# Storing before loading in every second full chunk of a streaming 1x1 convolution

One core of a Trainium2 chip. The metric is the device time of one execution, in microseconds (us), median of several runs.

## The reference

```python
x:  (1, 384, 384, 384) bf16;  dw: (1, 1, 384) bf16;  pw: (384, 384) bf16
out = x * dw[0, 0]                            # k = 1: one factor per channel
return einsum('bhwc,cd->bhwd', out, pw)       # a 147456 x 384 by 384 x 384 product
```

The kernel folds `dw` into `pw` once and then streams `x` through: 113 MB in, 113 MB out.

## The kernel before

The rows are cut into 42 chunks: sizes 1, 1, 2, 4 at the head, thirty-four full chunks of 8 supertiles (512 rows each), and 4, 2, 1, 1 at the tail. Full chunks are t = 4 to 37. VectorE transposes a supertile (X to T), TensorE multiplies it (T to PSUM), ScalarE and VectorE evict it (PSUM to O). SyncE issues all loads and stores of x and of the output, in program order, into one queue. X and O have three buffers each.

```python
LMAX = 8; NX = 3; NO = 3
def load_x(t):                       # chunk t into X[t % NX]
    d = nc.sync.dma_start(Xs[t % NX]..., src)   # je (here and below): the chunk's last supertile; its line is cut
    if t >= NX:                      # waits until chunk t-NX has been transposed
        d._wait_ge(s_t[je % 2][1], je // 2 + 1)
    d.then_inc(s_x[t % NX], 16)
def store(t):                        # O[t % NO] out; waits for the evictions of chunk t
    nc.sync.wait_ge(s_d[je % 2], je // 2 + 2)
    d = nc.sync.dma_start(dst, Os[t % NO]...)
    d._wait_ge(s_a[je % 2], je // 2 + 2)
    d.then_inc(s_o[t % NO], 16)
# ... cut: first loads, weights ...
for t in range(NT):
    if t + NX < NT:
        load_x(t + NX)
    store(t)
# ... cut: matmuls, transposes, evictions.
#     Transposes of a chunk wait for s_x; its first evictions wait for s_o.
```

## Time and profile before

| | before |
|---|---|
| time | 586.65 us, 3 runs (586.26 to 586.95) |
| span of the profile | 584.0 us |
| TensorE, VectorE busy | 97%, 97% |
| DMA | 1.01 of its engines' time from 200 to 300 us, 406 GB/s |

The prediction shows the lines for these. One view it does not show is the list of waits (who waited for whom: us in total, times, longest):

```profile
DVE T L174 <- DMA X<-in_x_dram: 1.6, 2, 1.3
PE ps L134 <- DVE T L174: 1.0, 1, 1.0
```

Read it with the chain: the DMA is as full as TensorE, yet VectorE waits for a load only twice, for 1.6 us. The loads arrive ahead of need.

### The profile page before, as it was taken

To read this page: it belongs to the slowest core of one execution; us is meant where nothing else is said; L and a number is where in the kernel's file an instruction comes from. 1 tells how busy PE (TensorE), PEld (TensorE's weight loads), DVE (VectorE), ACT (ScalarE), POOL (GpSimd) and SP (SyncE) were. 2 spreads that over 40 slices of the span, in tenths; PEclk is the share of its full clock that TensorE was granted. 3 is DMA by queue.
4 is the path that set the end of the run, shared out by engine and by line. 5 is a ranking of instruction groups with operands and counts; after the bars stand their busy time and mean duration, and the time that the engine had idled before them with its cause. 6 is when DMAs were issued, how large, how long until landed. Compare 5 with 4: busy or idle time off the path is not lost.

```text
span 584.0 us, 29852 instructions
## 1 busy us (share of the span) xinstructions
PE 563.9 (97%) x13824; PEld 412.6 (71%) x13824; DVE 563.9 (97%) x876; ACT 326.9 (56%) x297; POOL 0.3 (0%) x5
## 2 busy tenths in 40 slices
PE   1999999999999999999999999999999999999995
PEld 0667777777777777777777777777777777777773
DVE  3899999999999999999999999999999999999995
ACT  3555555555555656565655555555555555555553
POOL 0000000000000000000000000000000000000000
PEclk9999999999999999999999999999999999999998
DMA  8799999999999999999999999999999999999858
GB/s 289 253 424 425 428 422 421 410 396 404 402 396 411 378 412 411 394 402 413 391 407 395 414 414 396 404 419 396 404 397 403 389 424 397 389 403 407 333 221 311
DMA packets 29277, 227.79 MB, mean 390 GB/s; under 512 B 1616, under 2 KB 5456, under 8 KB 24656
## 3 DMA queue, kind: packets, MB, share of 16 engines
q1 hardware_dynamic: 28640, 227.09, 97.1%
q10 hardware_dynamic: 624, 0.59, 0.4%
q14 instruction: 12, 0.10, 0.0%
q8 instruction: 1, 0.02, 0.0%
HBM read 114.43 MB, written 113.25 MB: 390 GB/s over the span
## 4 chain that ended last, share of the span: by engine, by line
PE 93%; DMA 5%; ACT 1%; SPq 0%; issue 0%; DVE 0%; ACTq 0%; DVEq 0%
PE ps L134 93%; DMA X<-in_x_dram 2%; DMA out_dram<-O 1%; DMA pw_r<-in_pw_dram 1%; ACT O L215 1%; ACT w_r L199 1%; DVE T L174 0%; SPq L89 0%; SPq L107 0%; SPq L95 0%; SPq L245 0%; DVEq L173 0%; ACTq L211 0%; ACTq L194 0%; SPq L84 0%
## 5 line engine op out<-in xcount | busy, mean ns | idle before, releaser
L134 PE MATMUL ps<-w_r,T 32*128 32x384 bf16 x13824 | 563.9, 322 | 13.8 <-ACT w_r L199 12.8
L134 PEld LDWEIGHTS ps<-w_r,T 32*128 32x128 bf16 x13824 | 412.6, 93 | 164.8 <-issue 14.4
L215 ACT CAST O<-ps 128x1152 bf16<-128x1152 f32 x288 | 322.2, 1119 | 245.2 <-PE ps L134 243.3
L174 DVE STREAM_TRANSPOSE T<-X 128x384 uint32<-128x384 uint32 x576 | 449.1, 856 | 1.6 <-DMA X<-in_x_dram 1.6
L212 DVE CAST O<-ps 128x384 bf16<-128x384 f32 x288 | 160.7, 558 | 6.8 <-PE ps L134 4.6
L199 ACT ACTIVATE w_r<-pw_r,dwsel 128x384 bf16<-128x384 bf16 x6 | 3.1, 601 | 5.4 <-DMA pw_r<-in_pw_dram 5.4
L186 DVE CAST dwsel<-dwt 32x12 f32<-32x12 bf16 x4 | 0.7, 163 | 3.9 <-DMA dwt<-in_dw_dram 3.8
L197 DVE TENSOR_SCALAR w_r<-pw_r,dwsel 128x384 bf16<-128x384 bf16 x6 | 1.5, 312 | 2.1 <-DMA pw_r<-in_pw_dram 2.1
L160 ACT ACT_TABLE_LOAD x1 | 1.3, 1283 | 2.3 <-issue 2.3
L157 DVE MEMSET seed<- 128x1 f32 x2 | 0.1, 59 | 1.0 <-SPq L84 1.0
L160 ACT COPY warm<-warm 128x1 f32<-128x1 f32 x2 | 0.3, 190 | 0.0
L234 POOL MEMSET const-bfloat16-1.0<- 128x1 bf16 x1 | 0.1, 102 | 0.0
L234 POOL MEMSET const-uint8-127<- 128x1 uint8 x1 | 0.1, 101 | 0.0
L158 POOL MEMSET warm<- 128x3 f32 x1 | 0.1, 100 | 0.5 <-SPq L84 0.5
L234 POOL MEMSET const-float32-0.0<- 128x1 f32 x1 | 0.1, 98 | 0.2 <-issue 0.2
L234 POOL MEMSET const-float32-1.0<- 128x1 f32 x1 | 0.1, 98 | 0.0
## 6 DMA issues: line engine op xcount, KB each, us to landing
X<-in_x_dram SPq DMA_DIRECT2D x34, 3072.0 KB, 17.9
out_dram<-O SPq DMA_DIRECT2D x34, 3072.0 KB, 23.0
X<-in_x_dram SPq DMA_DIRECT2D x2, 1536.0 KB, 12.4
out_dram<-O SPq DMA_DIRECT2D x2, 1536.0 KB, 13.5
X<-in_x_dram SPq DMA_DIRECT2D x4, 384.0 KB, 5.7
X<-in_x_dram SPq DMA_DIRECT2D x2, 768.0 KB, 10.1
out_dram<-O SPq DMA_DIRECT2D x4, 384.0 KB, 3.8
out_dram<-O SPq DMA_DIRECT2D x2, 768.0 KB, 11.3
```

What stands on the lines that cost most here:

```text
L134: mm = nc.tensor.matmul(PS[s][:, q, :D], lhsT=Ts[s][32 * q : 32 * q + 32, b, par::2], rhs=w_r[32 * q : 32 * q + 32, b, par, :], start=(b = ...
L157: nc.vector.memset(seed[:, s : s + 1], 0.0).then_inc(s_d[s])
L158: nc.gpsimd.memset(warm[:], 0.0).then_inc(s_seed)
L160: c = nc.scalar.copy(warm[:, s + 1 : s + 2], warm[:, 0:1])
L174: ins = nc.vector.transpose(out=Tw[:, 3 * h : 3 * h + 3], in_=Xw[:, :, j, 96 * h : 96 * h + 96].rearrange("p k (b w) -> p b k w", w=32),)
L186: nc.vector.tensor_copy(dwsel[32 * q : 32 * q + 32, :], dwt[:].rearrange("w b r -> w (b r)")).then_inc(s_ds)
L197: i = nc.vector.tensor_scalar_mul(w_r[:, b, r, :], pw_r[:, b, r, :], sc)
L199: i = nc.scalar.activation(w_r[:, b, r, :], pw_r[:, b, r, :], COPY, scale=sc)
L212: e = nc.vector.tensor_copy(Ov[:, 3, j, :], PS[s][:, 3, :D])
L215: a = nc.scalar.copy(Ov[:, 0:3, j, :], PS[s][:, 0:3, :D])
L234: nc = _bacc.Bacc("TRN2", target_bir_lowering=False, num_devices=1)
```

## The change

The intent: two transfers of one kind follow each other in the queue, so there are half as many switches between reading and writing HBM. For full chunks with even t the store is issued first.

```diff
         for t in range(NT):
+            late = chunks[t] == LMAX and t % 2 == 0
+            if late:
+                store(t)
             if t + NX < NT:
                 load_x(t + NX)
-            store(t)
+            if not late:
+                store(t)
```

The queue's order goes from L S L S to S L L S S L L S. The even chunks' loads, called late loads below, stand behind the store's waits.

## The prediction

> **What bounds the kernel now.** I read the page first (busy shares, the chain that ended last, the groups), then the chain in order of time, the windows (is the DMA full?), SyncE's own timeline (when is each transfer issued?), and the DMA view window by window (when does each land?). The chain says where the end comes from:
>
> ```profile
> span 584.0 us, 29852 instructions
> PE 563.9 (97%) x13824; PEld 412.6 (71%) x13824; DVE 563.9 (97%) x876; ACT 326.9 (56%) x297; POOL 0.3 (0%) x5
> PE 93%; DMA 5%; ACT 1%; SPq 0%; issue 0%; DVE 0%; ACTq 0%; DVEq 0%
> L134 PE MATMUL ps<-w_r,T 32*128 32x384 bf16 x13824 | 563.9, 322 | 13.8 <-ACT w_r L199 12.8
> ...
> 31.44 538.40 PE ps L134 x13248
> ...
> 571.01 7.67 DMA out_dram<-O
> ```
>
> From 31.44 to 569.84 us the chain is nothing but matmuls: one unbroken piece of 538.40 us. The group's idle column says the same: 13.8 us of idle in all, 12.8 of them before the weights were scaled at the start. So the steady state is paced by TensorE (VectorE, 97% busy, turns with it), and not by any transfer. But the DMA has nothing to spare either:
>
> ```profile
> 200.00:300.00 100.00, 100.00 (x2468) 73.47 (x2464) 100.00 (x154) 57.55 (x52) 0.00 (x0) 1.00 1.01 406
> ```
>
> The last two columns are the DMA share and GB/s: 1.01 and 406 in the middle of the run (398 to 424 in the windows from 60.6 to 500). The demand is one full load and one full store (3072 KB each, 6.29 MB together) per full chunk of 15.60 us, or 403 GB/s. Two resources are full; only one of them ends the run. What lies between them is buffer slack, so I measured it. SyncE's timeline for chunks 34 (first two lines), 35 and 36:
>
> ```profile
> 513.43 0.33 SPq L95 DMA_DIRECT2D X<-in_x_dram  x1
> 516.41 0.39 SPq L107 DMA_DIRECT2D out_dram<-O  x1
> 529.03 0.33 SPq L95 DMA_DIRECT2D X<-in_x_dram  x1
> 532.01 0.39 SPq L107 DMA_DIRECT2D out_dram<-O  x1
> 544.63 0.33 SPq L95 DMA_DIRECT2D X<-in_x_dram  x1
> 547.61 0.39 SPq L107 DMA_DIRECT2D out_dram<-O  x1
> ```
>
> The load of chunk t+3 goes out at a moment I call a, when chunk t's transposes end; the store of chunk t follows 2.98 us later, when its evictions end. The pair repeats every 15.60 us. In the DMA view (size, us from issue to landing), window 44.5 to 60.1 (chunk 4), then 512.5 to 528.1 (chunk 34):
>
> ```profile
> X<-in_x_dram SPq DMA_DIRECT2D x1, 3072.0 KB, 13.6
> out_dram<-O SPq DMA_DIRECT2D x1, 3072.0 KB, 18.9
> ```
> ```profile
> X<-in_x_dram SPq DMA_DIRECT2D x1, 3072.0 KB, 20.0
> out_dram<-O SPq DMA_DIRECT2D x1, 3072.0 KB, 25.4
> ```
>
> Landings drift from 13.6 to 20.0 (loads) and from 18.9 to 25.4 (stores) over 30 chunks, about 0.21 us per chunk. The transfers are slower than TensorE by that much, 15.8 us a pair against 15.6, and the three-deep buffers absorb it. A load issued at a is wanted when chunks t+1 and t+2 have been transposed, at a + 31.2; it lands at a + 20.0 at worst, 11.2 us early. A store frees a buffer wanted about 32 us after its issue (the next writer of that buffer is three chunks on); it lands after 25.4 at worst, some 6.6 us early. That is why VectorE waits on loads for 1.6 us in the whole run, at the start and in the tail.
>
> **What the Trainium skill says.**
> 1. "Perfetto Trace Analysis", section Identifying the Most-Contended Engine: matmul busy time is no good measure of headroom, because matmuls are pipelined. So I don't rest on the 97%, but on the missing idle time and the fixed rhythm (evictions start every 1.95 us, at 291.02, 292.97, 294.92). The trace agrees: 322 ns for one matmul, while 48 of them take 1.95 us.
> 2. "DMA: Bandwidth & Descriptors", section Queues, rings and completion order: on each DMA engine descriptors are consumed in ring order, and a transfer is complete only when every engine it uses has reported. The trace agrees as far as it goes: every store lands after the load issued 2.98 us before it (at 2.98 + 25.4 = 28.4 against 20.0 for chunk 34, 8.4 us apart).
> 3. Same page, section Where 436 GB/s comes from: a ceiling of 435 GB/s for a core's DMA. The highest window reads 424, so halving the switches between loads and stores has at most some 3% to win on the DMA itself (estimate, 435/424), 8% against the demand of 403.
> 4. I found no page that puts a price on a switch from reading to writing HBM within a queue. The prediction has to get by without one.
>
> **The change, part by part.** Nothing is removed or added: 42 loads and 42 stores, with the same bytes, waits and buffers; TensorE, VectorE and ScalarE keep their instruction order. Only SyncE's order changes, for full chunks with even t: t = 4, 6, ... 36, 17 of the 34. The sequence L S L S becomes S L L S S L L S.
> - *The moved loads.* Load t+3 now stands behind the store's two waits, so it goes out at a + 2.98 + about 0.4 (the store's issue, 0.39), and in the ring it lies behind 3 MB that used to lie behind it. The bytes up to the end of the pair are the same, so the pair finishes when it did, with the load last: at a + 2.98 + 18.9 = a + 21.9 for chunk 4, and a + 28.4 for chunk 34. That is 8.3 to 8.4 us later than before. The deadline stays a + 31.2. Slack falls from 11.2 to **2.8 us** for the load issued at chunk 34, the worst full one (ready at 541.8, wanted at 544.6). It is 9.3 us at chunk 4. No wait: 0 us.
> - *The moved stores.* They go out at the same time and land earlier by about the time of one load (some 7.5 us, estimate: 3.15 MB at about 420 GB/s). No engine waits for them in the steady state: 0 us.
> - *The odd chunks.* Load t+4 and store t+1 are issued when they were, behind the same bytes as before: 0 us.
> - *Could the queue run dry in the longer gap before an even chunk?* At chunk 4, SyncE issues at 48.41 and the store before it (issued 32.45, 19.3 to land) lands at 51.75. At chunk 6 it issues at 79.61, and the store of chunk 5 (64.01 + 19.4) lands at 83.4. The small first store shows that a landing includes about 2 us that are not transfer (384 KB in 2.9 us), so 1.3 to 1.8 us of work are still queued at the leanest places, and more later. No dry spell: 0 us.
> - *The last moved load* (chunk 36, 768 KB) now lands no later than where store 36 landed, 547.61 + 16.5 = 564.1; it is wanted when chunk 38 is transposed, at 568.03 (SyncE issues the next load then). 3.9 us to spare: 0 us.
> - *The tail.* From 560.23 on the issues are the same in order and content. The 2.2 us that VectorE waits for a store near the end (and ScalarE 1.9) stay.
>
> Sum: 0 us, hence the time of before, 586.65, with a small allowance upward for the thin slack: **586.8 us**.
>
> **The rivals.**
> *A: fewer switches make the DMA faster.* For it: the DMA is full (1.01), and its landings drift. Against it: no compute engine waits for it between 31.44 and 569.84, so a faster DMA only ends the drift. It can shorten the wait for the last stores (7.67 us on the chain, of which ScalarE's idle before its last eviction is 1.9). At most about 2 us: 584.5.
> *B: the thin slack breaks.* If the new order makes a pair slower by more than 2.8/30 = 0.09 us, the loads of even chunks come late near the end and VectorE waits. The kernel is then DMA-bound, and self-limiting: every further 0.1 us per pair costs some 3 us over 30 pairs. A drift of 0.4 instead of 0.2 us gives about 3 us in waits and up to 3 in the tail: 590 to 592. For it: a margin of 2.8 us in 31.2 is not much, and two stores in a row could pile up at HBM. Against it: the bytes and descriptors are the same, and the three-deep buffers cover it on the measured numbers.
> *C: the change turns the kernel clearly DMA-bound.* Over 2% is 11.7 us, so the pair would have to slow by about (2.8 + 11.7)/30 = 0.48 us, 3% of the DMA's rate. Nothing in the trace points to it. 598 or more.
> *D: the late load stalls at every even chunk.* That would need a landing of over 31.2 us; the estimate is 21.9 to 28.4. It would cost up to some us per even chunk; I give it next to nothing.
>
> **Range and chances.** A gain is capped at 2 us, since TensorE's unbroken 538 us remain; a loss is open, but has to eat the slack first. Runs of before spread from 586.26 to 586.95. So the range is lopsided: 585.4 to 589.0. Faster by over 2% (below 574.9) would take a shorter matmul chain: 1%. Slower by over 2% (above 598.4) is rival C: 3%. Within 2%: 96%.
>
> **What would show it.** In the changed kernel's profile the chain should still hold one piece of about 538 us of matmuls; VectorE's waits on loads should stay near 1.6 us; loads of even chunks should land some 19 to 25 us after their later issue, their stores in about 11 to 18, and odd chunks should keep 13.6 to 20 and 19 to 25. The DMA share should stay at 1.00 with about 403 GB/s. I am wrong if VectorE waits for loads in the last third (B), if those waits come from chunk 7 on (D), if TensorE's piece breaks up and GB/s drop below 395 (C), or if landings stop drifting and the time falls by 1 to 2 us (A).

## The result

594.9 us (4 runs, 593.97 to 594.97) against 586.75 us (4 runs) of the kernel before, a ratio of 1.0136 (95% interval 1.0119 to 1.0154). Ratios here are the mean time of one kernel's fast runs over that of the other's of the same rounds, so not quite the ratio of the medians quoted. The change costs 1.4%: within 2%, but well above the predicted range.

The page of the changed kernel: span, busy shares, and the chain that ended last by engine.

```profile
span 593.2 us, 29852 instructions
PE 565.0 (95%) x13824; PEld 412.8 (70%) x13824; DVE 562.9 (95%) x876; ACT 327.0 (55%) x297; POOL 0.3 (0%) x5
DVE 54%; DMA 25%; PE 15%; issue 4%; ACT 1%; SPq 0%; DVEq 0%; ACTq 0%
```

The busy times are those of before; the span is 9.2 us longer. The chain has left TensorE. Its DVE share must be read with care: TensorE and VectorE run in step, and the chain follows now one, now the other. The new thing is the 25% of DMA. In order of time (start, us, what), the longest DMA pieces late in the chain are:

```profile
361.89 28.79 DMA X<-in_x_dram
393.24 30.00 DMA X<-in_x_dram
425.79 29.49 DMA X<-in_x_dram
...
490.29 29.56 DMA X<-in_x_dram
...
577.17 10.76 DMA out_dram<-O
```

In the kernel before this stretch was one piece of 538.40 us of matmuls. Now the chain goes through late loads, each 28.8 to 30.0 us long, and ends in a store that takes 10.76 us instead of 7.67. The waits:

```profile
DVE T L179 <- DMA X<-in_x_dram: 9.6, 6, 3.6
PE ps L139 <- DVE T L179: 8.6, 7, 3.2
```

VectorE waits 9.6 us for loads, TensorE in turn 8.6 us for VectorE. By the trace, 1.8 us of the 9.6 lie at the start (1.3 in the kernel before), 4.2 between 390 and 520 us, and 3.6 at 584 us, before the last chunk. Where is the time lost? The windows give the DMA share and GB/s in their last columns. The kernel before from 400 to 500 us, then the changed kernel in two windows:

```profile
400.00:500.00 100.00, 100.00 (x2471) 73.52 (x2464) 100.00 (x155) 57.39 (x52) 0.00 (x0) 1.00 1.01 405
```
```profile
200.00:300.00 100.00, 100.00 (x2472) 73.75 (x2464) 100.00 (x155) 57.21 (x52) 0.00 (x0) 1.00 1.01 405
400.00:500.00 100.00, 97.09 (x2384) 71.10 (x2379) 96.07 (x149) 55.76 (x50) 0.00 (x0) 1.00 0.98 387
```

Until 300 us nothing is lost. From 400 to 500 us TensorE is idle for 2.9 us and the DMA moves 387 GB/s instead of 405. The issue times split the 9.2 us. SyncE's timeline of the changed kernel (x2 is two issues: the first at the start given, the second at its end):

```profile
377.05 16.14 SPq L107 DMA_DIRECT2D out_dram<-O  x2
393.24 12.89 SPq L95 DMA_DIRECT2D X<-in_x_dram  x2
408.75 16.98 SPq L107 DMA_DIRECT2D out_dram<-O  x2
425.79 12.89 SPq L95 DMA_DIRECT2D X<-in_x_dram  x2
```

Two chunks took 31.2 us before; from 393.24 to 425.79 they take 32.55. The store of chunk 25 goes out at 377.05 against 376.01 before, 1.0 us later, and that 1.0 us was there at the fourth store already (33.49 against 32.45), so it arose in the head. In other runs that fourth store goes out anywhere from 32.2 to 33.9 us, so I count it as scatter. The store of chunk 37 goes out at 569.37 against 563.21, 6.2 us later: 5.1 us were lost between chunks 26 and 37. From there to the end it is another 3.1 us (the span differs by 9.2 in all). So: **1.0 head, 5.1 in the stretch in which late loads are missed, 3.1 tail**.

Why were the loads late? The DMA view, from issue to landing, of the changed kernel: the store of chunk 5, then that of chunk 25.

```profile
out_dram<-O SPq DMA_DIRECT2D x1, 3072.0 KB, 20.0
```
```profile
out_dram<-O SPq DMA_DIRECT2D x1, 3072.0 KB, 29.4
```

The same store of chunk 25 in the kernel before, with the load issued ahead of it:

```profile
X<-in_x_dram SPq DMA_DIRECT2D x1, 3072.0 KB, 19.1
out_dram<-O SPq DMA_DIRECT2D x1, 3072.0 KB, 24.6
```

Chunks 5 and 25 are odd: their store was issued in the old order and at the old phase, behind the same bytes. Before, its delay grew from 19.4 to 24.6 us, 0.26 us per chunk; now from 20.0 to 29.4, 0.47 per chunk. The DMA itself has become slower, 4.8 us by chunk 25, and the prediction's sum leaves a late load 3.8 us of slack at chunk 24 (31.2 - 2.98 - 24.4) and 2.8 at chunk 34. VectorE first waits for the late load of chunk 24 (0.66 us, at 390.77). The first to miss clearly is chunk 26's; its store and load land after

```profile
out_dram<-O SPq DMA_DIRECT2D x1, 3072.0 KB, 22.0
X<-in_x_dram SPq DMA_DIRECT2D x1, 3072.0 KB, 30.0
```

and the timeline has VectorE standing still for it:

```profile
423.33 1.55 DVE L179 STREAM_TRANSPOSE T<-X 128x384 uint32<-128x384 uint32 x2 [1.51 <-DMA X<-in_x_dram]
```

393.24 + 30.0 = 423.24; the transposes start at 423.33 after 1.51 us of idle.

**Which transfers got longer?** Transfers land in the order of their issue, so the step from one landing to the next tells what each one costs the engine that finishes last. In us, from the landings in the trace, in two stretches of both kernels (the changed kernel's order is S L L S):

```
before, issued 139.03 to 157.61:   L 7.65  S 8.39  L 7.68  S 8.41      sum 32.1
before, issued 295.03 to 313.61:   L 7.32  S 8.36  L 7.30  S 8.40      sum 31.4
after,  issued 143.05 to 158.65:   S 8.41  L 7.28  L 8.13  S 8.41      sum 32.2
after,  issued 299.05 to 314.65:   S 8.44  L 7.93  L 7.31  S 8.42      sum 32.1
```

Stores cost 8.4 everywhere. The whole difference is in the loads: before, they settle at 7.3; in the changed kernel one of the two stays at about 8. The demand is one such set of four per 31.2 us, so in the later stretch the new order falls 0.9 us behind per two chunks where the old one falls 0.2.

### The profile page after: what moved, and what is told of

Its sections match the earlier page's. It is cut to its first block, busy times and chain, and to the rows that moved or that the text cites. A ratio compares the mean times of both kernels' runs of the same rounds, so it can differ in the third digit from the quotient of the medians.

```text
span 593.2 us, 29852 instructions
## 1 busy us (share of the span) xinstructions
PE 565.0 (95%) x13824; PEld 412.8 (70%) x13824; DVE 562.9 (95%) x876; ACT 327.0 (55%) x297; POOL 0.3 (0%) x5
## 4 chain that ended last, share of the span: by engine, by line
DVE 54%; DMA 25%; PE 15%; issue 4%; ACT 1%; SPq 0%; DVEq 0%; ACTq 0%
DVE T L179 43%; DMA X<-in_x_dram 22%; PE ps L139 15%; DVE O L217 10%; DMA out_dram<-O 2%; DMA pw_r<-in_pw_dram 1%; ACT O L220 1%; ACT w_r L204 1%; SPq L107 0%; SPq L89 0%; SPq L95 0%; DVEq L178 0%; SPq L105 0%; SPq L250 0%; ACTq L216 0%
```

## The experiments

Two theories to begin with. **P (pairing):** a run of two loads makes the DMA slower. **Q (lateness):** it is the late issue, or the two issues back to back. The kernels of one batch ran on one chip, with the kernel before beside them (586.4 to 586.9 in each batch).

### All full chunks late

```diff
-            late = chunks[t] == LMAX and t % 2 == 0
+            late = chunks[t] == LMAX
```

> Every full chunk stores first and loads second (S L S L): all loads are late, but no two transfers of one kind follow each other. Theory P (pairing: in a run of two loads the slowest DMA engine loads while the other fifteen load as well, and its load takes 0.5 to 0.9 us longer): no pairs, so landings drift as before (stores end near 15 to 18 us after issue, loads land at most 28.4 us after the moment the chunk's transposes end), VectorE waits for loads about 1.6 us as in the kernel before, time 586 to 588.5. Rival Q (lateness or two issues back to back cost the DMA time, whatever the order): twice as many late loads as in the changed kernel, so waits from about chunk 14 on and a time of 598 to 605.

588.89 us, ratio 1.0045 (1.0028 to 1.0061). Load steps average 7.38 us to 375 us and 7.30 after: the old pace, with every load late. That speaks against Q. The time is just above the range expected; VectorE waits 2.3 us once near the end, for the load of chunk 40, which was issued at chunk 37, behind that chunk's store.

### The same without late loads in the tail

```diff
+            late = chunks[t] == LMAX and t < 36
```

> S L S L as in the first experiment, but chunks 36 and 37 load first again. If that run's 2.4 us over the kernel before came from the two late loads of the tail (it waited 2.3 us once, for the load of chunk 40), this one is at 586 to 587: late loads alone, without two of a kind in a row, cost nothing. If lateness costs something by itself, 588 to 589.

586.81 us, ratio 0.9998 (0.9983 to 1.0014). Thirty-two loads 3 us later and behind their stores cost nothing measurable, so long as kinds alternate and the tail is left alone. So in this order lateness costs nothing, and lateness alone does not explain the change's loss.

### Old order, late issue

```diff
+            if chunks[t] == LMAX and t % 2 == 0:
+                je = s0[t] + chunks[t] - 1
+                nc.sync.wait_ge(s_d[je % 2], je // 2 + 2)
+                nc.sync.wait_ge(s_a[je % 2], je // 2 + 2)
             if t + NX < NT:
                 load_x(t + NX)
             store(t)
```

> Even full chunks wait for their evictions, then issue load and store back to back, load first: the order in the queue is that of the kernel before (L S L S), only the issue of every second load is 3 us later. Theory P (pairing): drift as before, no waits in the steady state, 586 to 587.5. Rival Q (late, back-to-back issue): the landing of odd stores drifts to 29 to 30 us as in the changed kernel, time 589 to 595.

589.97 us, ratio 1.0061 (1.0044 to 1.0078). A miss for P as I had put it: there are no pairs, yet load steps average 7.82 us before 215 us (7.51 in the kernel before). After that they are 7.38, then 7.29, as before. The backlog gained early stays, and in the tail VectorE waits 3.1 us for a load. So something other than pairs can make loads longer, for a while. The time lies in the range given for Q (589 to 595), although the store of chunk 25 lands after 27.5 us, short of Q's 29 to 30: in the old order a late issue does cost something.

### Old order again after chunk 20

```diff
+            late = chunks[t] == LMAX and t % 2 == 0 and t <= 20
```

> The changed order only up to chunk 20, then load first again. Drift theory: by chunk 20 the queue is some 3.5 us further behind than before and stays there, but loads go out on time again with 11 us of slack, so no waits in the steady state; the tail is 2 to 3.5 us longer: 588 to 590.5. If lateness alone cost time, without a growing backlog, the time is that of before, 586 to 587.5.

596.49 us, ratio 1.0163 (1.0146 to 1.018): slower than the change itself, and outside every expectation. (The profiled run took 600.77, the other four 595.78 to 596.89.) From chunk 21 on the order and issue are the old ones, but load steps average 7.67 (215 to 375 us) and 8.04 (375 to 525 us), and the stores' delay climbs to 36.1 us. Evictions then wait for O buffers, 20.3 us in total for ScalarE. A theory that only pairs cost cannot explain this.

### Four X buffers under the change, and under the kernel before

```diff
-NX = 3
+NX = 4
```

> The changed kernel with four X buffers instead of three: a load has 46.8 us instead of 31.2. Theory P and Q alike say that the DMA's drift stays (odd stores land later by about 0.47 us per chunk, beyond 30 us by chunk 27) and that VectorE's waits for loads vanish; what is left is the longer tail (about 3 us) and, if the stores pass their own deadline of about 32 us near chunk 31, a few us of waits for stores: 588 to 592. If the loss did not come from late loads at all, the time stays at 594 to 596.

> The kernel before with four X buffers. It separates the buffer from the order in the earlier run of the changed kernel with four X buffers (585.6). If that run's gain of 0.9 us over the kernel before came from the buffer (last loads go out a chunk earlier, so less is queued ahead of the last stores), this one is 583.5 to 586; if from the order, this one is 586.5 like the kernel before.

The change with four X buffers takes 585.6 us, ratio 0.9986 (0.997 to 1.0003). The stores' delay still grows, from 21.0 at chunk 5 to 28.9 at chunk 25 and 32.2 at chunk 33, and load steps average 7.6. But the waits for loads are gone from the list altogether. It did better than I expected: the tail is shorter too, the last store of the chain taking 7.33 us instead of 10.76, since the last loads go out a chunk earlier. This shows what the slow DMA costs and how: nothing until a load misses its time.

The kernel before with four X buffers takes 584.78 us, ratio 0.997 (0.9956 to 0.9984). So the small gain came from the buffer. Whether the order takes part of it back is not shown: the two intervals overlap. With the last version below, which takes as long, this is the best measured, by 0.3%.

### The DMA alone, in both orders

All compute removed, output zeros, so wrong. 36 loads and 36 stores of 3072 KB; each waits only for the transfer of three chunks before in its buffer.

```diff
+            late = PAIR and t % 2 == 0        # PAIR: False in the one, True in the other
+            if late: put(t)                   # shortened; load and put are the transfers
+            if t + NX < NF: load(t + NX)
+            if not late: put(t)
```

> No compute, wrong result on purpose (the output is zeros): 36 loads and 36 stores of 3072 KB, order L S L S, each waiting only for its buffer's transfer of three chunks before. It measures the DMA alone. At the 7.3 us per load and 8.4 us per store by which landings follow each other in the kernel before: 36 x 15.7 = 565 us plus some 10 us at the ends, 570 to 580.

> The same with the changed order S L L S. Theory P1 (pairing of loads costs the DMA time by itself): 17 pairs x 0.5 to 0.9 us, so 8 to 15 us more than the alternating twin. Rival R (pairing costs nothing by itself; the longer loads of the changed kernel come from how the sixteen engines stand to each other when the issues are timed by the compute): within 3 us of the twin, or faster.

561.81 us alternating (560.95 to 562.41; I expected 570 to 580, with stores at 8.4 us, and they step by 7.4 here), 568.16 us in pairs (567.96 to 568.8). So the pairs cost 6.35 us over 18 even chunks, 0.35 us each, with no compute and no compute-timed issue. That is less than the 8 to 15 I expected, and clearly not nothing. The pages give

```profile
HBM read 113.25 MB, written 113.25 MB: 404 GB/s over the span
```
```profile
HBM read 113.25 MB, written 113.25 MB: 400 GB/s over the span
```

for the alternating and the paired kernel. The intent of the change, fewer switches and hence a faster DMA, fails at its root: on this pattern pairing makes the DMA slower by 1.1%.

The trace's record of single DMA packets says a little more. A load moves in 128 packets of 24,576 bytes, 912 ns each in most records, a store in 512 of 6,144 bytes, 234 ns in most. I counted packets in flight on the sixteen engines (times from the span's start):

```
alternating:  mostly 12 loads beside 4 stores, or 4 beside 12 (280 to 315 us)
paired:       0 loads, 16 stores from 280 to 287; 16 loads, 0 stores from 294 to 302.5;
              at 301.5 to 303.5, just ahead of the stores, load packets of 1.0 to 1.9 us
```

Alternating, the engines spread over both kinds. In pairs, all sixteen do the same thing, and the loads at the end of the run stretch to up to twice their length. Why they do is not shown.

### Where the slowest engine stands

The same count in the full kernels shows that one of the sixteen engines is behind: in the kernel before at 308.5 to 311.5 us, one load packet is in flight beside fifteen or so stores. This is the engine whose finish sets the landing (the load lands at 313.17). In the changed kernel at 314 to 317.5 us, where the one store packet in flight is its own, such packets take 248 to 286 ns where the others' take 234. That fits the steps: stores step by 8.4 us here and by 7.4 in the DMA-only kernel.

The trace shows this engine without any count of packets. A transfer's semaphore is raised sixteen times, and the landing is the sixteenth. (Point 2 of the prediction rests on this. The page has it not in the section named there but in a later one, Why a DMA increments its semaphore by 16 and not by 1: only the full count means that all data has landed.) For the load issued at 295.03 in the kernel before, fifteen increments come 10.1 to 13.5 us after the issue and the last after 18.1. For the late load issued at 299.50 in the changed kernel they come at 16.5 to 16.9, and the last at 26.5. From chunk 5 to chunk 34 the gap between the fifteenth and the last grows from 0.6 to 6.8 us in the kernel before, and from 1.0 to 11.8 in the changed one; the fifteenth's own delay in the kernel before is 13.2 us at both ends. And 6.3% of that kernel's store packets, one in sixteen, take 248 to 300 ns. So the drift that the prediction read as the transfers being slower than TensorE is that of one engine of sixteen (that it is the same one throughout is inferred).

In the settled kernel before, it lies about one transfer behind, so it loads while the others store. In the changed kernel from 317.5 to 323 us it loads while all the others load (16 loads, 0 stores), and around 320 to 322 us load packets on the engines take 1.1 to 1.7 us instead of 0.91. The load that lands then (issued 299.50) has a step of 7.93.

For every full load of the changed kernel after 60 us I took the mean number of load packets in flight during its step (both ends moved 1.0 us earlier, my estimate of the delay from last byte to landing):

```
loads in flight   loads   mean step
0 to 4              10      7.32 us
4 to 14             13      8.08 us     (a change of kind among the others falls in the step)
14 to 16             7      7.49 us
```

This gave a third theory. **R (position):** a load costs the last engine more when the other fifteen are loading during part of it; a run of two loads is one way to get there, a backlog of more than one transfer another. I thought that it fitted the late-issue run (loads longer only while the last engine was not yet a transfer behind) and the return at chunk 21 (the last engine was then too far behind, and its loads came beside the next loads of the others).

The same count for another run speaks against R as it is worded. In the kernel with all loads late to chunk 35, the other engines are loading when each of the 30 full loads from 60 to 525 us begins its step, and storing when it ends (4.7 to 13.2 load packets in flight on average). Yet 29 of them take 7.28 to 7.41 us, and one 8.01. Loads beside the step, and a change of kind within it, are therefore not enough to make a load longer.

The kernel with half the pairs and the one that starts late:

```diff
+            late = chunks[t] == LMAX and t % 4 == 0              # every fourth chunk
+            late = chunks[t] == LMAX and t % 2 == 0 and t >= 24  # from chunk 24
```

> The changed order at every fourth chunk only (8 or 9 pairs instead of 17). Drift theory: half the pairs, half the added backlog, about 4 us by chunk 36; loads of late chunks land up to 31.5 us after the transposes' end, waits at most 1 to 2 us near the end, tail 2 to 3.5 us longer: 588.5 to 591.5. If pairs were not what costs, about half of 8.2 us would not be expected; 586.5 to 587.5 then.

> The changed order only from chunk 24 on. Drift theory (each pair of loads costs the slowest engine about 0.5 us): 7 pairs by chunk 36 add about 3 us to a backlog that is 4.8 us smaller at chunk 24 than in the changed kernel; the late loads land 28.5 to 31 us after the transposes' end, so at most 1 us of waits, and the tail is 2 to 3 us longer: 588.5 to 591. If a late load costs the same at any backlog, 6 late full loads of 17 give a third of the 8.2 us: 589 to 590 as well, but with waits of 2 us or more.

Half the pairs: 594.16 us, ratio 1.0113 (1.0091 to 1.0135), nearly the full loss. A miss: the delay of the store of chunk 25 is 28.6 us, nearly that with all pairs (29.4), and loads outside the pairs take 8.0 us as well (8.03 at the load issued at 327.34, 8.00 at 389.74; others stay at 7.3). The loss does not go by the number of pairs. From chunk 24 on: 590.46 us, ratio 1.0057 (1.0037 to 1.0077); load steps average 7.36 us from 215 us to chunk 23, and 7.64 from there. It meets the expectation in time and in its waits: of 5.5 us of waits for loads, 2.4 lie at the start, before the change acts, 3.1 in the tail, and none between.

### Only the backlog changed

The cause was still open (pairs or position), so three more kernels ran. The first keeps the old order and issue, and puts one extra load of 3072 KB into the queue at chunk 8, into a spare buffer that nobody reads.

```diff
+            if t == 8:
+                nc.sync.dma_start(spare, xf[:4096]...).then_inc(s_spare, 16)
                 # cut: the spare tile, its semaphore, a wait for it at the very end
             if t + NX < NT:
                 load_x(t + NX)
             store(t)
```

> The kernel before, with one extra load of 3072 KB into a spare buffer put into the queue at chunk 8 (read by nobody, result correct); order and issue times otherwise those of before. All engines get 7.3 us more work once. Position theory: the slowest engine is then a whole load further behind, and its loads come to lie beside the other engines' loads: the mean step from a store's landing to the next load's landing rises from 7.4 to 7.6 or more, stores pass 32 us after issue around chunk 20 to 25, and evictions wait: 592 to 600. Pair theory: steps stay at 7.3 to 7.4, stores start at 27 and end at 32 to 33 us, waits of at most 1 us, tail up to 6 us longer: 588 to 593, steps unchanged.

602.62 us (599.07 to 606.16), ratio 1.0274 (1.022 to 1.0329), above both ranges expected. Load and store of chunk 10, and of chunk 26:

```profile
X<-in_x_dram SPq DMA_DIRECT2D x1, 3072.0 KB, 22.7
...
out_dram<-O SPq DMA_DIRECT2D x1, 3072.0 KB, 28.1
```
```profile
X<-in_x_dram SPq DMA_DIRECT2D x1, 3072.0 KB, 30.0
out_dram<-O SPq DMA_DIRECT2D x1, 3072.0 KB, 35.4
```

The extra load itself lands 7.3 us after its predecessor. From chunk 8 to chunk 14 load steps are 7.3 and the delay of the stores stays (27.9 to 28.5 us). Then, from about 29 us of delay on, steps of 7.6 and later of 8.0 and more appear, with no pair in the program but the extra load itself; some steps of 7.2 lie between them at first, and the average after 375 us is 8.14. ScalarE ends up waiting:

```profile
ACT O L221 <- DMA out_dram<-O: 27.2, 13, 5.0
```

7.3 us of extra transfer cost 16 us. So a larger backlog alone is followed by longer loads, and pair theory as the only cause falls. That position is what does it (R) is not shown: here too, the load issued at 107.55 begins its step beside sixteen loads, the one at 201.15 ends beside fourteen, and both take 7.3 us.

### Stopping early

```diff
+            late = chunks[t] == LMAX and t % 2 == 0 and t <= 10
```

> Changed order only at chunks 4, 6, 8 and 10, old order after. Position theory (a load costs the slowest engine more only when the other fifteen load during it): about 2 us of added backlog at chunk 11; the old order then goes on at its old pace (7.3 to 7.5 us per load) as long as a store lands within some 25 us, and near the end, past that, loads cost 7.7 and more: 587.5 to 590. Pair theory (only pairs cost): 2 us more backlog to the end, no further growth beyond the old 0.2 us per chunk: 587 to 588.5. If a start in the changed order spoils the whole run as chunks 4 to 20 did: 595 or more.

587.11 us, ratio 1.0018 (1.0001 to 1.0035). After the four pairs the loads go back to 7.30 and 7.29; the last full stores land after 25.9 us. The time is in the range given for the pair theory (587 to 588.5) and below that of position (587.5 to 590), which wanted loads of 7.7 us past 25 us of delay. In this run that backlog was harmless. There is no one threshold, though: the late-issue run kept 7.3 us up to 28.2 us of delay, and the kernel with half the pairs had loads of 8.0 us at 27. The mean load steps of the main kernels in one table (us, by time of issue):

| kernel | 60 to 215 | 215 to 375 | 375 to 525 | time |
|---|---|---|---|---|
| before | 7.51 | 7.36 | 7.29 | 586.7 |
| all late to chunk 35 | 7.31 | 7.36 | 7.30 | 586.8 |
| change to chunk 10 | 7.67 | 7.30 | 7.29 | 587.1 |
| old order, late issue | 7.82 | 7.38 | 7.29 | 590.0 |
| the change | 7.77 | 7.61 | 7.69 | 594.9 |
| change to chunk 20 | 7.88 | 7.67 | 8.04 | 596.5 |
| before + one load | 7.33 | 7.64 | 8.14 | 602.6 |

### The tail

```diff
+            late = chunks[t] == LMAX and t % 2 == 0 and t <= 34
```

> The changed kernel without its last late load (chunk 36 loads first again, as before). If the 3.6 us wait for that load is a loss of its own, the time falls by about 3 us, to 591 to 592.5. If what the tail loses is set by the backlog of the stores behind which everything lands, the next wait takes its place and it stays at 593.5 to 595.

594.98 us, ratio 1.0161 (1.0135 to 1.0187), no gain. The load of chunk 39 now lands at 564.09 instead of 573.67, and the total of waits for loads stays at 9.3 us. The run aimed at the wrong load: the wait of 3.6 us is for the last load, which is issued at 574.18 in the changed kernel and lands at 583.94, just behind the store of chunk 37; it is there in this run too (3.54 us). VectorE never waited for the load of chunk 39. That the tail's loss is set by the backlog fits this, but the run removed no wait and so does not show it.

### Looking for a better version

```diff
-NO = 3                                                           # kernel before
+NO = 4
```

```diff
-NX = 3                                                           # all late to chunk 34
+NX = 4
```

> The kernel before with four O buffers instead of three: the last evictions need not wait for the store of three chunks back (VectorE waited 2.2 us for it, ScalarE 1.9). 584 to 585.5 if that wait is on the end's path; 586.5 if the last store lands no earlier because it queues behind the others anyway.

> S L S L up to chunk 34 with four X buffers: stores go ahead of loads, loads have 47 us. No two of a kind in a row. It should do what the kernel before does with four X buffers (584.8), 584 to 585.5, with stores landing some 8 us sooner and no waits in the steady state; a candidate for the best version, but I expect no gain over that one, because TensorE's chain is the same.

A fourth O buffer under the kernel before: 586.99 us, ratio 1.0005 (0.9991 to 1.0019), the second of the two cases expected: waits for stores are gone from its list, but the last store lands at 582.38 against 582.60 in the kernel before. All late to chunk 34 with four X buffers: 585.08 us, ratio 0.9966 (0.995 to 0.9981), the same as the kernel before with four X buffers, as expected. Four buffers for both did not fit in SBUF (the build asks for 198 KB per partition and has 189.7) and were not built further.

## Why the prediction was wrong

- **The bound: right.** TensorE paces the steady state and the DMA is as full; both orders keep 97% until buffers miss their time, and with four X buffers the new order shows no wait for loads.
- **The step that failed:** "The bytes up to the end of the pair are the same, so the pair finishes when it did, with the load last". The bytes are the same; the time they take is not. One load of each pair took about 8 us where both had settled at 7.3, and the delay of an odd store grew by 0.47 us per chunk instead of 0.26. Equal bytes behind equal gates were taken for equal time, and for the odd chunks ("behind the same bytes as before: 0 us") likewise.
- **The margin: right in kind.** Early late loads landed as worked out: the one issued at 49.90 landed 17.9 us later, 21.4 us after the transposes' end, against a predicted 21.9. I put the break at 0.09 us more per chunk; it was 0.21 more (0.47 - 0.26), which by chunk 24 is 4.2 us against a slack of 3.8. This is rival B, which I named and gave too little weight.
- **Rival B's size: about right, its drift too small.** For a drift of 0.4 I gave about 3 us of waits and up to 3 in the tail. By the same rule (3 us per further 0.1) a drift of 0.47 gives about 5. Measured: 5.1 and 3.1, with 1.0 of scatter in the head. Of rival C's signs both came, a broken TensorE piece and less than 395 GB/s (387), but not its time.
- **Rival A, fewer switches make the DMA faster: wrong in sign.** The DMA alone took 6.35 us more in pairs.
- **Backlog.** I assumed that a backlog keeps its pace. The extra-load run shows that it need not: there, past some 29 us of delay, the same order turns 7.3 us loads into 8 us ones.

What stays open: what makes a load of the last engine stretch. Pairs do it in the DMA-only kernel and a larger backlog does it without pairs, but no count of packets made here tells the long loads from the short ones in all runs. And why one engine's stores are slower (248 to 286 ns a packet) only while the compute runs. The runs with an added buffer also move the addresses of the buffers behind it, which no run controls for; before the extra load was issued, that kernel's steps were those of the kernel before.

## What to carry to other kernels

When two resources are full and buffers stand between them, compare the growth of delay over the run with the slack left, and treat the growth as something that the change itself can alter. Moving a transfer later is only free if the queue's pace is unchanged; look at the landings of the transfers that were not moved to see whether it is. In the DMA-only kernels alternating let the sixteen DMA engines spread over both directions, and grouping cost 1.1%. And look at the single increments of a transfer's semaphore before calling the DMA full or slow: in the full kernels here one engine of sixteen set the landings.

## What the Trainium skill lacked or had wrong

- "DMA: Bandwidth & Descriptors": no section says what the order of loads and stores in one queue is worth. Here 36 + 36 transfers of 3 MB took 561.81 us alternating and 568.16 us in pairs.
- The same page, section Latency and other measured facts, says that DMA engines 7 and 15 are usually slower, and ties its best guess at the cause to the software descriptor path. In these runs, with the stream's transfers issued by SyncE only, one engine's stores were slower as well (8.4 us a store against 7.4), and only while the compute ran. Which engine it was, the trace does not tell, so it is not shown that it is one of those two.
- No page says that a larger backlog can slow the transfers that follow: 7.3 us of extra transfer cost 16 us (602.62 against 586.37).
